# Block 4's gate and val by quarters as seven products in two shared PSUM banks, and sums of weights made from tiles already loaded

## Chip, cores and metric

One core of a Trainium2 chip. The metric is the time of one execution on the device in microseconds (us), the median of the runs shown. All data is fp32; a product of two fp32 matrices is made on TensorE from high and low parts (`float32r`): hi*hi + hi*lo + lo*hi, three matmuls.

## What is computed

Three stages over 3072 tokens of width 512 (batch 4, 8 heads, sequence 768, head size 64):

```python
# 1 retention, per head, gamma fixed by the head
state = gamma * state + outer(k[t], v[t]);  y[t] = scale * q[t] @ state
# 2 gated MLP, d_ff 1536
xn = x / sqrt(mean(x * x) + 1e-6) * rms_g
x2 = (silu(xn @ w_gate) * (xn @ w_val)) @ w_out
# 3 second MLP, d_ff 1024
h = x2 @ w_in;  solu = h * softmax(h)
out = layernorm(solu) * g_ln @ w_out2
```

## The kernel before

The tokens go in six blocks of 512 (`NB`), each through two stages on TensorE. The first stage makes gate, val and their output product over 12 pieces m of d_ff (`NM`), 128 wide; the second stage (`de_quarters` from block 2 on) is the second MLP, and ends with four output products (`e_mm`). While block n is in its first stage, the attention of block n + 1 runs between, in eight pieces (`att_pieces`: a score piece and an output piece for each of four chunks), in PSUM banks SB and YB. These pieces, the RMS norm of the next block, loads and other side work hang on numbered slots: `slot(n, s)` is called at slot 0 to 34 in the first stage (three to a piece m) and 35 to 57 in the second, and runs the functions that `extra` holds for it. Written order is not final: the planner of the framework orders each engine's instructions by its own times, within the ties that `issue_after` sets. Each engine, and SyncE's DMA queue, runs its instructions in that order.

In blocks 0 to 4 the first stage is `bc_block`: for each m, `gv` (L805) makes gate into bank GB and val into VB, each 4 k x 3 matmuls of 512 columns, `act_hl` (L814) multiplies silu(gate) by val and splits it, and `cmm` (L825) adds the output product of the piece before to the four banks X0 to X3, 12 matmuls. Weights are in DRAM as high and low part (`scr[m][part]`, 512 KB each; part 0 gate, 1 val, 2 output), written in block 0 and loaded again by `w_load` for each block: gate and val into four `w4` tiles, output weights into two `wo` tiles.

Block 5 (`SEVEN`) has another first stage, `seven_block` (L943). Two pieces m go together as a pair j, and each of gate and val is a 2 x 2 product of quarters (256 inputs or outputs by 256 tokens) by a Strassen-like scheme with seven products in place of eight. Each product is `seven_mm`, six matmuls of 256 columns (L913). Four products come in a first phase (`seven_1`) and three in a second (`seven_2`), into four quarters a, b | c, d: two halves of GB and two of VB for gate, SB and YB for val, since block 5 has no attention beside it. VectorE adds the quarters up between (L926 to L941, L973, L980). The products need sums of quarters of the weights and of the activations.

Sums of weights: for each j and part `sums_steps` (L586) loads two weight tiles, adds high and low part (L597), makes four sums on GpSimd (L605), splits them and stores them in DRAM (`sscr`), two loads and two stores of 512 KB. `SUMS_AT` puts these twelve jobs into block 2 (slots 17, 24), 3 and 4 (slots 1, 7, 13, 19, 25). `seven_load` and `seven_pump` fetch quarters and sums in tiles of a ring of ten and two.

Sums of activations: `x_sums` (L452) makes four differences in place in xT on GpSimd (L464), and their splits and those of three known quarters, in the slots 50 to 53 of block 4, that is beside its `e_mm`. The normalised activations live in xnh and xnl, where the second stage also keeps T weights that `t_load` brings. Low parts of these splits are made by GpSimd too (L101), high parts by ScalarE (L100).

Of the kernel before, what the change touches and what calls it, by code (L numbers as in the profile page):

```python
# [9 lines left out]
F32 = mybir.dt.float32  # L10
# [8 lines left out]
P = 128  # L19
# [16 lines left out]
SEVEN = (5,)  # L36
SUMS_AT = [(2, 17), (2, 24)] + [(n, 1 + 6 * i) for n in (3, 4) for i in range(5)]
# [5 lines left out]
def retention_moe_kernel(ctx: ExitStack, tc: tile.TileContext, qk0, q2, kt, kv, wpk, w2i, w2o,  # L43
# [395 lines left out]
    def rms_steps(bank, n):  # L439
        if n == 1:  # L440
            return [first(lambda: rms_1(bank)), first(lambda: rms_2(bank))] \
                + [first(lambda k=k: rms_mul(bank, k)) for k in range(NK)] \
                + [lambda k=k: xn_split(k) for k in range(NK)]
        norm = [rms_1t, lambda: rms_sum(bank), rms_2t] + [lambda k=k: rms_3t(k) for k in range(NK)]
        if n in SEVEN:
            return norm + x_sums()
        return norm + [lambda k=k: xn_split_t(k) for k in range(NK)]
# [4 lines left out]
    def x_sums():  # L452
# [10 lines left out]
        def sub(a, b, out):  # L463
            return lambda: nc.gpsimd.tensor_tensor(out=out, in0=a, in1=b, op=ALU.subtract)  # L464

        def summed(key, src, tag):
            def f():
                xs[key] = tuple(wt(tag, [P, 2, 256], F32R, 2) for _ in range(2))
                split(*xs[key], src, nc.gpsimd)
            return f  # L470

        k01, k23 = slice(0, 2), slice(2, 4)
        return [known("B11", k01, lo), known("B21", k23, lo), known("B22", k23, hi),
                sub(b12, b11, b11), sub(b22, b12, b12), sub(b22, b11, b22), sub(b21, b22, b21),
                summed("T2", b22, "rq"), summed("T3", b12, "rk"), summed("T1", b11, "kd"), summed("T4", b21, "qd")]
# [110 lines left out]
    def sums_steps(j, part):  # L586

        W, f, o = [], [], []

        def load():  # L590
            for m in (2 * j, 2 * j + 1):
                W.append(wt("x2", [P, 2, 512], F32, 4))
                nc.sync.dma_start(W[-1], scr[m][part])

        def whole():
            for w in W:
                nc.gpsimd.tensor_tensor(out=w[:, 0, :], in0=w[:, 0, :], in1=w[:, 1, :], op=ALU.add)  # L597

        def sums():
            a11, a12, a21, a22 = W[0][:, 0, lo], W[0][:, 0, hi], W[1][:, 0, lo], W[1][:, 0, hi]  # L600
            f.extend((st(), st()))
            s2, s3, s1, s4 = f[0][:, lo], f[0][:, hi], f[1][:, lo], f[1][:, hi]
            for out, a, b, op in ((s1, a21, a22, ALU.add), (s2, s1, a11, ALU.subtract),
                                  (s3, a11, a21, ALU.subtract), (s4, a12, s2, ALU.subtract)):
                nc.gpsimd.tensor_tensor(out=out, in0=a, in1=b, op=op)  # L605

        def parts():
            for t in f:
                o.append(wt("x2", [P, 2, 2, 256], F32R, 4))
                with tc.issue_after(recent["act"].ins), tc.issue_after(recent["dve"].ins):  # L610
                    split(o[-1][:, :, 0, :], o[-1][:, :, 1, :], t.rearrange("p (s x) -> p s x", s=2))

        def store():
            for i, t in enumerate(o):
                nc.sync.dma_start(sscr[j][part][:, 2 * i:2 * i + 2], t.bitcast(F32))

        def none():
            pass

        return [load, none, whole, sums, none, none, parts, none, store]  # L620
# [184 lines left out]
    def gv(g, part):  # L805
        w = wsp.pop((g, part))
        halves = [slice(0, 256), slice(256, 512)] if g == 0 else [slice(0, 512)]
# [17 lines left out]
    def cmm(g, m):  # L825
        w = wsp.pop((g, 2))
        ah, al = acts.pop(m)
        for d in range(NK):
            cs = slice(d * P, d * P + P)
            mm3(XB[d], w[:, 0, cs], w[:, 1, cs], ah, al, m == 0, m == NM - 1)  # L830
# [77 lines left out]
    def seven_mm(ps, w, key, start):  # L908
        h, l = xs[key]
        for k in range(2):  # L910
            cs = slice(k * P, k * P + P)
            for i, (x, y) in enumerate(((w[:, 0, cs], h), (w[:, 0, cs], l), (w[:, 1, cs], h))):
                nc.tensor.matmul(ps, lhsT=x, rhs=y[:, k, :], start=start and k + i == 0, stop=k == 1 and i == 2,  # L913
                                 skip_group_check=True)
# [28 lines left out]
    def seven_block(n):  # L943
        base = n * NM
        for j in range(NM // 2):
# [39 lines left out]
            if final:  # L985
                out(m - 1)
        t_load(0, n)
# [418 lines left out]
    for n in range(NB):  # L1406
        if n + 1 < NB:
# [4 lines left out]
            else:  # L1412
                begin, span, r = 0, 28, (30, 32, 33, 34, 34, 34, 34, 50, 50, 51, 51)
                extra.setdefault((n, 31), []).append(lambda n=n: t_load(0, n))
# [7 lines left out]
            if n + 1 in SEVEN:  # L1422
                r = (30, 32, 33, 34, 34, 34, 34, 50, 50, 50, 51, 51, 51, 51, 52, 52, 53, 53)
                first7 = [lambda: seven_load(n + 1)] \
                    + [lambda i=i: w_load((n + 1) * NM + i, 2) for i in range(2)] + [seven_pump]
                for s, f in zip((47, 48, 48, 51), first7):
# [7 lines left out]
            for i, (b, s) in enumerate(SUMS_AT):  # L1434
                if b == n:
                    for k, f in enumerate(sums_steps(i // 2, i % 2)):
                        extra.setdefault((n, s + k), []).append(f)
        (seven_block if n in SEVEN else bc_block)(n)
# [82 lines left out]
```

## Time and profile before

| | us |
|---|---|
| median of three runs | 981.66 |
| the runs | 974.83, 981.66, 981.83 |
| the profiled execution, whole | 975.58 |
| its span, first to last instruction | 973.5 |

The views name an instruction by engine and line: PE is TensorE's matmuls, PEld its weight loads, DVE VectorE, ACT ScalarE, POOL GpSimd, SPq SyncE's DMA queue. A matmul's own duration in a timeline includes its latency; what it costs in a stream is the distance between starts, which is also what the chain of waits gives. The granted clock of TensorE is 0.991 of full speed over the span.

### The profile page before, as it was taken

To read this page: it belongs to the slowest core of one execution; us is meant where nothing else is said; L and a number is where in the kernel's file an instruction comes from. 1 tells how busy PE (TensorE), PEld (TensorE's weight loads), DVE (VectorE), ACT (ScalarE), POOL (GpSimd) and SP (SyncE) were. 2 spreads that over 40 slices of the span, in tenths; PEclk is the share of its full clock that TensorE was granted. 3 is DMA by queue.
4 is the path that set the end of the run, shared out by engine and by line. 5 is a ranking of instruction groups with operands and counts; after the bars stand their busy time and mean duration, and the time that the engine had idled before them with its cause. 6 is when DMAs were issued, how large, how long until landed. Compare 5 with 4: busy or idle time off the path is not lost.

```text
span 973.5 us, 17543 instructions
## 1 busy us (share of the span) xinstructions
PE 957.4 (98%) x6636; PEld 797.4 (82%) x6636; DVE 522.9 (54%) x1036; ACT 407.8 (42%) x792; POOL 450.1 (46%) x490
## 2 busy tenths in 40 slices
PE   8899999999999999999999999999999999999998
PEld 7777887888887888888888888788888888999987
DVE  4787777563375653734473343475433366343473
ACT  3767655474244343322463222356222246321254
POOL 6886764683053484644535345627253336300022
PEclk8899999999999999999999999999999999999999
DMA  9699999896523305999823999932799953798501
GB/s 346 224 316 397 343 325 367 294 390 237 202 63 98 99 23 182 303 301 312 309 98 111 293 347 345 346 128 93 241 328 328 328 187 130 236 326 296 192 1 44
DMA packets 89044, 231.93 MB, mean 238 GB/s; under 512 B 11136, under 2 KB 28928, under 8 KB 87936
## 3 DMA queue, kind: packets, MB, share of 16 engines
q1 hardware_dynamic: 80176, 205.63, 63.1%
q10 hardware_dynamic: 8784, 25.17, 6.7%
q8 instruction: 53, 0.87, 0.4%
q14 instruction: 31, 0.25, 0.1%
HBM read 188.82 MB, written 41.94 MB: 237 GB/s over the span
## 4 chain that ended last, share of the span: by engine, by line
PE 82%; DMA 5%; POOL 5%; DVE 4%; ACT 3%; issue 1%; SPq 0%; ACTq 0%; POOLq 0%; DVEq 0%
PE X L801 9%; PE X L803 9%; PE X L802 9%; PE GB L801 6%; PE GB L803 6%; PE GB L802 6%; PE VB L801 5%; PE VB L802 5%; PE VB L803 5%; PE X L1184 3%; PE SB L121 3%; PE GB L1184 2%; PE VB L1184 2%; PE VB L913 2%; PE YB L913 2%; PE X L1043 1%
## 5 line engine op out<-in xcount | busy, mean ns | idle before, releaser
L802 PE MATMUL X<-r,wo 128*128 128x512 f32 x260 | 101.8, 392 | 0.0
L803 PE MATMUL X<-r,wo 128*128 128x512 f32 x260 | 101.2, 390 | 0.0
L820 DVE TENSOR_TENSOR f<-VB,f 128x512 f32<-128x512 f32 x60 | 41.3, 688 | 111.2 <-PE VB L803 96.0
L801 PE MATMUL X<-r,wo 128*128 128x512 f32 x260 | 99.1, 395 | 1.9 <-DMA wo<-scr 1.4
L100 ACT CAST r<-f 128x512 fp32r<-128x512 f32 x72 | 44.6, 620 | 130.5 <-DVE f L820 112.3
L702 POOL TENSOR_TENSOR st<-st,x 128x512 int32<-128x512 int32 x52 | 69.8, 1344 | 54.3 <-DVE st L701 19.3
L849 ACT ACTIVATE f<-GB 128x512 f32<-128x512 f32 x60 | 35.8, 596 | 129.7 <-PE GB L803 128.7
L801 PE MATMUL GB<-xnh,w 128*128 128x512 f32 (+1 forms) x220 | 86.9, 395 | 1.0 <-ACT xnh L403 1.0
L801 PE MATMUL VB<-xnh,w 128*128 128x512 f32 (+1 forms) x220 | 86.5, 393 | 0.0
L802 PE MATMUL GB<-xnl,w 128*128 128x512 f32 (+1 forms) x220 | 85.9, 391 | 0.3 <-DVE xnl L101 0.2
L803 PE MATMUL VB<-xnh,w 128*128 128x512 f32 (+1 forms) x220 | 85.5, 389 | 0.0
L802 PE MATMUL VB<-xnl,w 128*128 128x512 f32 (+1 forms) x220 | 85.5, 389 | 0.0
L803 PE MATMUL GB<-xnh,w 128*128 128x512 f32 (+1 forms) x220 | 85.4, 388 | 0.0
L101 DVE TENSOR_TENSOR r<-f,r 128x512 fp32r<-128x512 f32 x72 | 65.2, 907 | 31.3 <-ACT r L100 30.6
L281 POOL TENSOR_TENSOR U<-U,u 128x256 f32<-128x256 f32 x27 | 17.1, 631 | 100.3 <-PE YB L121 76.7
L101 POOL TENSOR_TENSOR r<-st,r 128x512 fp32r<-128x512 f32 x8 | 10.3, 1292 | 112.6 <-ACT r L100 112.6
L801 PEld LDWEIGHTS X<-r,wo 128*128 128x128 f32 x260 | 48.5, 188 | 12.8 <-issue 2.2
L801 PE MATMUL X<-w2oh,r 128*128 128x512 f32 (+1 forms) x144 | 56.7, 394 | 1.1 <-ACT f L1086 0.6
L802 PEld LDWEIGHTS X<-r,wo 128*128 128x128 f32 x260 | 48.8, 188 | 10.4 <-DVE r L101 0.4
L803 PEld LDWEIGHTS X<-r,wo 128*128 128x128 f32 x260 | 48.8, 188 | 10.2
L597 POOL TENSOR_TENSOR x<-x 128x512 f32<-128x512 f32 x24 | 31.0, 1296 | 54.3 <-DMA x<-scr 54.2
L803 PE MATMUL X<-w2oh,r 128*128 128x512 f32 (+1 forms) x144 | 55.8, 387 | 0.0
(456 smaller groups left out, 2538.7 us busy)
## 6 DMA issues: line engine op xcount, KB each, us to landing
w<-scr SPq DMA_DIRECT2D x96, 512.0 KB, 6.6
wo<-scr SPq DMA_DIRECT2D x59, 512.0 KB, 6.5
x<-in_wpk SPq DMA_DIRECT2D x36, 512.0 KB, 6.3
x<-scr SPq DMA_DIRECT2D x25, 512.0 KB, 7.5
sscr<-x SPq DMA_DIRECT2D x24, 512.0 KB, 8.6
rv<-in_kv SPq DMA_DIRECT2D x40, 256.0 KB, 6.3
scr<-CV ACTq DMA_DIRECT2D x18, 512.0 KB, 6.7
scr<-w ACTq DMA_DIRECT2D x12, 512.0 KB, 5.6
```

What stands on the lines that cost most here:

```text
L100: h = nc.scalar.copy(hi, src)
L101: (lo_eng or nc.vector).tensor_tensor(out=lo, in0=src, in1=hi.bitcast(F32), op=ALU.subtract)
L121: return lambda: nc.tensor.matmul(out, lhsT=lhsT, rhs=rhs, start=start, stop=stop)
L597: nc.gpsimd.tensor_tensor(out=w[:, 0, :], in0=w[:, 0, :], in1=w[:, 1, :], op=ALU.add)
L702: nc.gpsimd.tensor_tensor(out=ti, in0=ti, in1=lo, op=ALU.add)
L801: nc.tensor.matmul(ps, lhsT=lh, rhs=rh, start=start, stop=False)
L802: nc.tensor.matmul(ps, lhsT=lh, rhs=rl, start=False, stop=False)
L803: return nc.tensor.matmul(ps, lhsT=ll, rhs=rh, start=False, stop=stop)
L820: recent["dve"] = nc.vector.tensor_tensor(out=a, in0=GV[1], in1=silu[:, 0, :], op=ALU.mult)
L849: recent["act"] = nc.scalar.activation(s[:, 0, :], GV[0], AF.Silu)
L913: nc.tensor.matmul(ps, lhsT=x, rhs=y[:, k, :], start=start and k + i == 0, stop=k == 1 and i == 2, skip_group_check=True)
L1184: last["mm"] = nc.tensor.matmul(bank, lhsT=x[:, k, ts_], rhs=y[:, k, :], start=start and k + i == 0, stop=k == 1 and i == 2, skip_group_ch ...
```

## The change

Block 4 is put in `SEVEN`. `seven_block` stays for block 5; block 4 gets `shared_block`, in which gate and val take the four quarters of GB and VB in turn, with one output product between phase one and phase two from the second pair on. Its weights come by quarters through `fit`, a ring of six tiles (four `w4`, two `x2`), each of two products' weights, refilled by two DMAs of 256 KB as soon as its second product is issued. The last two output weights go to other tiles, and the T weights are loaded after the block.

Ten of the twelve sums of weights are made from the weight tiles that the block in progress has loaded for its own products (`kept`): (j 3 and 4) in block 2, (j 0 to 2) in block 3; j 5 still loads them, in block 3 at slots 17 and 23. None is left in block 4. They are made in place, and stored by four DMAs of 256 KB.

The differences of activations go to tiles of their own (`wo`) and are made at slot 35; their splits come at slots 39 to 42 for block 5, and at 51, 52, 52 and 55 for block 4. The output scaling of block 3's last `e_mm` is not put off to block 4's first slot any more.

```diff
-SEVEN = (5,)
-SUMS_AT = [(2, 17), (2, 24)] + [(n, 1 + 6 * i) for n in (3, 4) for i in range(5)]
+SEVEN = (4, 5)
+SUMS = {2: [(3, 0), (3, 1), (4, 0), (4, 1)], 3: [(0, 0), (0, 1), (1, 0), (1, 1), (2, 0), (2, 1)]}
+LATE_SUMS = {(3, 17): (5, 0), (3, 23): (5, 1)}
...
+        def subs():
+            for keys in (("T2", "T3"), ("T1", "T4")):
+                t = wt("wo", [P, 2, 2, 256], F32, 2)
+                raws.update((key, t[:, i]) for i, key in enumerate(keys))
+            for key, a, b in (("T1", b12, b11), ("T2", b22, raws["T1"]), ("T3", b22, b12), ("T4", b21, raws["T2"])):
+                nc.gpsimd.tensor_tensor(out=raws[key], in0=a, in1=b, op=ALU.subtract)
...
+        def whole(i):
+            w = kept.pop((2 * j + i, part))
+            if not X:
+                X.append(wt("x2", [P, 2, 512], F32, 4))
+            nc.gpsimd.tensor_tensor(out=X[0][:, i, :], in0=w[:, 0, :], in1=w[:, 1, :], op=ALU.add)
...
+        if resident:
+            at0, at1 = 6 * j + part, 6 * j + 3 + part
+            return {at0: [lambda: whole(0)], at1: [lambda: whole(1), sums], at1 + 2: [parts], at1 + 3: [store]}
+        return {0: [load], 2: [both, sums], 4: [parts], 5: [store]}
...
+        def mul(j, part, q, ps, key, start=False):
+            seven_mm(ps, stock.pop((j, part, q)), key, start)
+            at = 14 * j + 7 * part + q
+            if at % 2 and at // 2 + len(fit) < NT:
+                fit_load([at // 2 + len(fit)])
+
+        def phase1(j, part):
+            for q, ps, key in ((0, a, "B11"), (1, b, "T2"), (2, c, "T3"), (3, d, "T1")):
+                mul(j, part, q, ps, key, q in (0, 2))
+            y, t = f4(), st()
+            S.copy(t[:, hi], b)
+            V.tensor_tensor(out=t[:, lo], in0=a, in1=t[:, hi], op=ALU.add)
+            V.tensor_tensor(out=t[:, hi], in0=c, in1=t[:, lo], op=ALU.add)
+            V.tensor_tensor(out=y[:, 1, hi], in0=d, in1=t[:, hi], op=ALU.add)
+            return y, t
+
+        def phase2(j, part, y, t):
+            for q, ps, key in ((4, a, "B21"), (5, d, "B22"), (6, c, "T4")):
+                mul(j, part, q, ps, key)
+            V.tensor_tensor(out=y[:, 0, hi], in0=d, in1=t[:, lo], op=ALU.add)
+            V.tensor_tensor(out=y[:, 1, lo], in0=c, in1=t[:, lo], op=ALU.add)
...
+        for j in range(NM // 2):
...
+            g = phase1(j, 0)
+            slot(n, 6 * j)
+            if j:
+                out(m - 2, range(1) if final else range(NK))
+            slot(n, 6 * j + 1)
+            phase2(j, 0, *g)
...
+            silu = S.activation(gf[:, 256:], gf[:, 256:], AF.Silu)
+            slot(n, 6 * j + 2)
+            v = phase1(j, 1)
+            slot(n, 6 * j + 3)
...
+            elif j:
+                out(m - 1)
+            slot(n, 6 * j + 4)
+            phase2(j, 1, *v)
...
+            V.tensor_tensor(out=vf[:, lo], in0=a, in1=gf[:, lo], op=ALU.mult)
+            V.tensor_tensor(out=vf[:, hi], in0=vf[:, hi], in1=gf[:, hi], op=ALU.mult)
...
+            slot(n, 6 * j + 5)
...
+                r += (39, 40, 41, 42) if n + 1 == NB - 1 else (51, 52, 52, 55)
...
+        (seven_block if n == NB - 1 else shared_block if n in SEVEN else bc_block)(n)
```

## Rows read from the trace of the kernel before

**Rows 1.** The page, part 1: TensorE's busy time, share of the span, instructions.

```profile
PE 957.4 (98%) x6636; PEld 797.4 (82%) x6636; DVE 522.9 (54%) x1036; ACT 407.8 (42%) x792; POOL 450.1 (46%) x490
```

**Rows 2.** Waits of TensorE in blocks 3 to 5: us in total, times, longest.

```profile
PE X L801 <- DMA wo<-scr: 1.4, 1, 1.4
...
PE X L801 <- ACT f L1086: 0.6, 1, 0.6
...
PE GB L913 <- DVE st L926: 0.3, 1, 0.3
```

**Rows 3.** Windows: length, then busy time per engine, granted clock, DMA share, GB/s.

```profile
632.93:785.90 152.97, 152.97 (x1143) 125.54 (x1143) 73.60 (x155) 54.35 (x111) 66.54 (x78) 1.00 0.72 243
785.90:924.56 138.66, 137.72 (x861) 123.83 (x861) 69.66 (x167) 50.35 (x100) 26.95 (x36) 1.00 0.65 225
...
522.00:632.90 110.90, 109.50 (x897) 89.35 (x889) 43.01 (x81) 29.95 (x60) 50.07 (x54) 1.00 0.96 314
675.50:785.90 110.40, 110.40 (x942) 90.32 (x941) 43.76 (x81) 29.82 (x60) 46.17 (x52) 1.00 0.90 302
837.35:924.56 87.21, 87.21 (x601) 81.29 (x602) 39.12 (x91) 20.46 (x40) 0.00 (x0) 1.00 0.82 282
```

**Rows 4.** Timeline of TensorE, block 3: start, duration; twelve matmuls of 512 columns begin.

```profile
622.92 0.39 PE L801 MATMUL VB<-xnh,w 128*128 128x512 f32 x1
...
625.64 0.39 PE L801 MATMUL X<-r,wo 128*128 128x512 f32 x1
```

**Rows 5.** The chain of waits, block 5: start, length; 48 products' matmuls begin.

```profile
857.44 1.42 PE GB L913 x12
...
863.09 0.23 PE X L801
```

**Rows 6.** Timeline of TensorE, block 4: a score piece and an output piece.

```profile
675.79 0.27 PE L121 MATMUL SB<-rq,rk 64*64 64x64 f32 x1
...
676.65 0.66 PE L1043 MATMUL X<-ident,f 128*128 128x128 f32 x4
...
713.68 0.27 PE L121 MATMUL SB<-qd,U 64*64 64x64 f32 x1
...
715.01 0.50 PE L801 MATMUL VB<-xnh,w 128*128 128x512 f32 x1
```

**Rows 7.** Line 913's weight loads: duration in ns, min/median/max.

```profile
L913 PEld LDWEIGHTS VB<-qd,A x36: 187/188/192, 839.6 to 913.9; 128*128 128x128 f32 x36
```

**Rows 8.** Timeline of TensorE, block 5: a second phase's last product.

```profile
871.99 0.87 PE L913 MATMUL YB<-qd,A 128*128 128x256 f32 x6
872.70 0.28 PE L913 MATMUL GB<-xnh,x 128*128 128x256 f32 x1
```

**Rows 9.** Timeline of VectorE, the same stretch.

```profile
871.54 0.42 DVE L973 TENSOR_TENSOR f<-SB,f 128x256 f32<-128x256 f32 x1 [2.75 <-PE SB L913]
872.90 0.42 DVE L939 TENSOR_TENSOR f<-YB,st 128x256 f32<-128x256 f32 x1 [0.93 <-PE YB L913]
873.24 0.41 DVE L980 TENSOR_TENSOR f<-YB,st 128x256 f32<-128x256 f32 x1
...
874.67 0.69 DVE L101 TENSOR_TENSOR r<-f,r 128x512 fp32r<-128x512 f32 x1
```

**Rows 10.** Groups of VectorE in block 4 that are attention's.

```profile
L349 DVE TENSOR_REDUCE ssq<-sq 128x128 f32<-128x512 f32 x4 | 4.3, 1087 | 3.4 <-ACT sq L346 3.4
...
L278 DVE TENSOR_TENSOR U<-U,YB 64x128 f32<-64x128 f32 x14 | 4.0, 287 | 0.2
```

**Rows 11.** DMA issues in block 5: size, median us to landing.

```profile
w<-sscr SPq DMA_DIRECT2D x7, 256.0 KB, 5.2
```

**Rows 12.** The chain of waits, end of block 3.

```profile
620.13 9.66 DMA wo<-scr
```

**Rows 13.** Groups of GpSimd in block 3: the adds of a weight's parts.

```profile
L597 POOL TENSOR_TENSOR x<-x 128x512 f32<-128x512 f32 x8 | 10.3, 1289 | 23.1 <-DMA x<-scr 23.1
```

**Rows 14.** Timeline of GpSimd before block 5: the last split.

```profile
833.25 1.29 POOL L101 TENSOR_TENSOR qd<-xT,qd 128x512 fp32r<-128x512 f32 x1
```

More of the change, by code (lines that the diff above doesn't have):

```diff
@@ L584, in retention_moe_kernel @@
     recent = {}
-    def sums_steps(j, part):
-        W, f, o = [], [], []
-        def load():
[L591 to L597, printed above, removed]
-        def sums():
[L600 to L604, printed above, removed]
+    kept = {}
@@ new lines, in sums_steps, with both @@
+    def sums_steps(j, part, resident):
+        X, H = [], []
+        def whole(i):
[3 more added lines that the diff above has]
+            nc.gpsimd.tensor_tensor(out=X[0][:, i, :], in0=w[:, 0, :], in1=w[:, 1, :], op=ALU.add)
+        def load():
+            for t, m in ((X, 2 * j), (H, 2 * j + 1)):
+                t.append(wt("x2", [P, 2, 512], F32, 4))
+                nc.sync.dma_start(t[0], scr[m][part])
+        def both():
+            for i, w in ((0, X[0]), (1, H[0])):
+                nc.gpsimd.tensor_tensor(out=X[0][:, i, :], in0=w[:, 0, :], in1=w[:, 1, :], op=ALU.add)
+        def sums():
+            a11, a12, a21, a22 = (X[0][:, r, c] for r in range(2) for c in (lo, hi))
+            for out, a, b, op in ((a22, a21, a22, ALU.add), (a21, a11, a21, ALU.subtract),
+                                  (a11, a22, a11, ALU.subtract), (a12, a12, a11, ALU.subtract)):
@@ L617, in none @@
-        def none():
-            pass
-        return [load, none, whole, sums, none, none, parts, none, store]
+            if not H:
+                H.append(wt("x2", [P, 2, 512], F32, 4))
+            with tc.issue_after(recent["act"].ins), tc.issue_after(recent["dve"].ins):
+                for i in range(2):
+                    split(H[0][:, i, :].bitcast(F32R), X[0][:, i, :].bitcast(F32R), X[0][:, i, :])
+        def store():
+            for i, t in enumerate((H[0], X[0])):
+                for r, to in ((0, slice(0, 4, 3)), (1, slice(1, 3))):
+                    nc.sync.dma_start(sscr[j][part][:, to, i, :], t[:, r, :].rearrange("p (s x) -> p s x", s=2))
@@ L806, in gv @@
         w = wsp.pop((g, part))
+        if (g % NM // 2, part) in SUMS.get(g // NM, ()):
+            kept[g % NM, part] = w.bitcast(F32)
         halves = [slice(0, 256), slice(256, 512)] if g == 0 else [slice(0, 512)]
@@ L986, in seven_block, with fit_load, source @@
                 out(m - 1)
+        t_load(0, n)
+        with tc.issue_after(recent["wo"].ins):
+            t_load(1, n), t_load(2, n)
+        out(NM - 2)
+        out(NM - 1)
+    fit, stock = [], {}
+    def fit_load(tiles):
+        def source(j, part, q):
+            if q in (0, 4, 6):
+                return scr[2 * j + (q == 6)][part][:, :, lo if q == 0 else hi]
+            return sscr[j][part][:, (1, 2, 3, 5).index(q)]
+        for T in tiles:
+            t = fit[T % len(fit)]
+            for i in range(2):
+                key = ((2 * T + i) // 14, (2 * T + i) // 7 % 2, (2 * T + i) % 7)
+                nc.sync.dma_start(t.bitcast(F32)[:, i], source(*key))
+                stock[key] = t[:, i]
```

124 lines of the change are left out of this document (91 added, 33 removed).

## The prediction

> **What bounds the kernel now.** I read the page's first part, then who waits for whom on TensorE, then the windows by stage, then the chain of waits, whose pieces give the distance between starts in place of a matmul's whole latency. The page shows TensorE busy for 98% of the span [rows 1]. The waits say that this is work and not smeared idle time: over blocks 3 to 5 TensorE waited three times, 1.4, 0.6 and 0.3 us [rows 2]. The windows agree: in block 4 (675.5 to 785.9 us) and in block 5 (837.35 to 924.56) TensorE is busy for all of it at granted clock 1.00, while VectorE, ScalarE and GpSimd are each busy for less than half [rows 3]. So in block 4 the time is the number of matmuls times their pitch, and an edit of another engine or of a DMA is worth nothing until it makes TensorE wait. DMA is nearest to that: share 0.96 in block 3, 0.90 in block 4 [rows 3].
>
> **The products (the gain).** Block 4 now takes gate and val with 12 x 2 x 4 x 3 = 288 matmuls of 512 columns. Twelve of them start at 622.92 and the next instruction at 625.64: 2.72 / 12 = 0.2267 us each [rows 4], so 65.3 us. By sevens it is 6 pairs x 2 parts x 7 products x 6 = 504 matmuls of 256 columns. Block 5 already runs them: 48 in a row from 857.44 to 863.09, 5.65 / 48 = 0.1177 us [rows 5], so 59.3 us. The gain is 6.0 us. In columns it would be one eighth, 8.2 us; the short matmul gives some back, since 0.1177 is more than half of 0.2267. A check from whole stages: from the start of one second stage to the next it is 152.97 us with block 4 between and 138.66 with block 5 [rows 3], 14.31 apart. Block 4 has four chunks of attention more, each a score piece of 0.86 us and an output piece of 1.33 [rows 6], 8.76 in all, and block 5's stage holds 0.95 us of waits [rows 2]: 14.31 - 8.76 + 0.95 = 6.5. I take 6.0 and keep 6.5 as the other end.
>
> [...] Block 5's matmuls have a weight load each of 0.188 us [rows 7], those 48 together 9.0 us in a stretch of 5.65, so the loads lie beside the matmuls. [...] If loads stood in line, it would be 504 x (0.1177 + 0.188) = 154 us against 288 x (0.2267 + 0.188) = 119: 35 us lost. The trace disagrees; I keep 0.01 for it below.
>
> **The borders in shared banks (a new wait).** Block 5 has two sets of quarters (GB with VB, SB with YB). In block 4 SB and YB belong to block 5's attention, so gate and val use GB and VB in turn, and before each next group of products VectorE and ScalarE must have read the last one. The tightest place is from the last product of one part (into VB) to the first group of the next, where no output matmuls lie between: one border inside each of 6 pairs and one between pairs, 11. Block 5 shows the times. Its six products into the last quarter end where the next matmul starts, at 872.70 [rows 8], and the reads of that bank start at 872.90 and 873.24; the second ends at 873.65 [rows 9]. The products of the quarter that is read at 872.90 had all started before 871.99 [rows 8]: the read waited for the product beside it in the same bank. After a border two products go to GB first (12 x 0.1177 = 1.41 us, to 874.11 on this scale) before VB is written again: 0.4 us spare. GB is clear too, since its last quarter is read from 871.54, early [rows 9]. At the next step the parts for the output matmuls must be there: the low part's subtraction ends at 875.36 [rows 9], 2.66 after the border; block 4's output matmuls come four products later (2.82), and the low part is read first by the second of them, at 3.05. So without attention nothing waits, with 0.4 us to spare. Where no output matmuls cover the step from phase one to phase two (pair 0), an attention piece of 0.86 or 1.33 us lies there. What comes in front of these reads on VectorE is attention's work: 0.42 x 2 masks, 0.28 x 8 state adds and a 1.09 reduce a chunk, about 2.1 us a piece, eight pieces. If none lands before a border it costs 0; if each does, 8 x (2.1 - 0.4) = 13.8 us. The adds and the reduce are in [rows 10]; the masks have the shape of the quarters' adds in [rows 9]. I take 1.0, near the lower end, because VectorE is busy for 43.76 of 110.4 us [rows 3] and block 5, whose VectorE work is the same without attention, has no wait from 837.35 on.
>
> [...] By columns alone one quarter would be read before the last product ends, and 0.8 us would be spare at a border; by the bank it is 0.4: the trace shows the second.
>
> **The weights' quarters.** Each product pair takes a 512 KB tile from a ring of six, refilled by two 256 KB DMAs. From a tile's release to its next use ten products and at least one output pass: 10 x 0.706 + 12 x 0.2267 = 9.8 us (7.1 plus an attention piece in pair 0). Such a DMA lands in 5.2 us at the median in block 5 [rows 11]: some 4 us spare, less the time that SyncE takes to issue the two. Bytes: 36 refills and 12 output weights of 0.524 MB, 2.6 MB of attention, 3.1 of the second stage's T weights: 30.9 MB. Block 4 moved 302 GB/s x 110.4 = 33.3 MB [rows 3], with five pairs' sums that now leave it. So nothing waits: 0. The other end: at block 5's 282 GB/s [rows 3] 30.9 MB take 109.6 us where TensorE's share of that window would be 104.4: +5.2. A single row of a crowded queue speaks for it, 9.66 us to landing [rows 12].
>
> **The sums, blocks 2 and 3.** Ten of twelve are now made by GpSimd from the weight tiles that TensorE is using, and lose their 1 MB loads; two keep them. Block 3 held five sums of 4 x 0.524 MB, and holds six of half that and two whole: 10.5 MB both times, so its share of 0.96 stays. What moves is when: the last store leaves at slot 28, not 33, so the wait of 1.4 us at the block's end for output weights [rows 2, 12] may go. GpSimd gets three sums more, each two adds of 1.29 us [rows 13] and four of half width, between 2.6 and 7.7 us and about 5.2: 50.07 + 15.6 = 66 of 110.9 us, hidden, though a weight tile is held until its add is done. A weight load that is late for that costs about what the late one cost, 1.4 us; I take three such as the bad end. Value -0.7, ends -1.4 and +4.2.
>
> **The two seams.** For block 5 four subtractions and four splits leave the seam for the second stage before it, where GpSimd is idle for long. In the trace the last of these splits runs from 833.25 to 834.54 [rows 14], and TensorE's 0.95 us of waits [rows 2] stand behind that queue (the output scaling waits for GpSimd's small ops). I expect them gone. For block 4 four splits of 512 columns become seven: up to the same 0.95 comes in, I take 0.5. Net -0.45, ends -0.95 and +0.95. What is left (the T weights loaded after the block, its last two output weights in other tiles, the scaling for block 3 not put off) is covered by at least 8 us of output matmuls: 0.
>
> **The sum.** -6.0 + 1.0 + 0 - 0.7 - 0.45 = -6.15 us. The profiled execution took 975.58 us, its span of 973.5 and 2.1 around it: 969.4. The runs shown are 974.83, 981.66 and 981.83, so a run falls near 975 or near 982, and the profile is one of the first kind. I put the step on the middle of the profiled 975.58 and the median 981.66, 978.62: **972.5 us**.
>
> **The rivals.** (1) DMA becomes the bound in block 4: for it the share of 0.90 and the 9.66 us landing; against it block 5, which takes the same quarters at 0.82 without a wait, and fewer bytes than before. It gives back 5.2: 977.7. (2) VectorE's attention work stands before the borders, and the kernel gets slower: place, the 11 borders and the output matmuls behind them; price up to 13.8 in place of 1.0, so 972.5 + 12.8 = 985.3; it decides from (6.15 + 1.0) / 11 = 0.65 us a border. For it: spare time of 0.4 against a single reduce of 1.09. Against it: VectorE is idle for most of the block, and the planner may put these ops after the reads. (3) Block 3 gets crowded: +4.2 in place of -0.7, 977.4; for it DMA at 0.96. (4) Weight loads in line: +35 on the products, 1013; against it [rows 5, 7].
>
> **Chances.** Forecast 0.62 (its own range 967 to 976), (1) 0.16, (2) 0.13, (3) 0.08, (4) 0.01. The range: the best ends together, -6.5 - 1.4 - 0.95 = -8.85, from 975.58 give 966.7; above, rivals 1 and 3 on the upper of the two kinds of run, 981.66 - 1, and a part of rival 2: 967 to 983. One per cent, about what a measurement of this kernel can tell from no change, is 9.8 us, more than any case gains. It is passed only if the median of before stands on the upper kind and that of after on the lower, half of the forecast's 0.62: 0.30. Slower by over 1% needs rival 2 at its full price or rival 4: 0.06. Within 1%: 0.64.
>
> **What would show it.** Right: from the second stage of block 3 to that of block 4 it takes about 147 us where it was 152.97 [rows 3], 504 matmuls of line 913's kind in it at a pitch near 0.118, TensorE's waits in it under 2 us together, the block 3 and seam waits of rows 2 gone or smaller. Rival 1 shows as TensorE waiting for w or x tiles from scr and sscr; rival 2 as waits of the first VB product, or of output matmuls, for VectorE; rival 3 as waits for w in block 3. The forecast is wrong if block 4's stage shrinks by less than 3 us, or if its waits exceed 3.

## The result, and the profile after

The changed kernel takes 987.57 us (median of 14 runs, 980.21 to 992.36), the kernel before 978.26 beside it (14 runs): a ratio of 1.0094, 95% interval 1.007 to 1.0118. It is 0.9% slower, and outside the range of 967 to 983. The profiled execution after spans 985.8 us where that of before spans 973.5: 12.3 us apart where the medians are 9.3 apart, since the profiled execution of before is one of its shorter ones (975.58 us). The account below is of these two executions.

First the page of after, its part 1 and the DMA line of part 2 [rows 1]:

```profile
PE 959.8 (97%) x6852; PEld 805.7 (82%) x6852; DVE 562.9 (57%) x1102; ACT 413.1 (42%) x807; POOL 466.1 (47%) x497
...
DMA packets 109160, 230.92 MB, mean 234 GB/s; under 512 B 12176, under 2 KB 51472, under 8 KB 108048
```

TensorE has 216 matmuls more (504 short for 288 long), as intended, and is busy 2.4 us longer in a span 12.3 us longer. So something waits. The windows say where. A stage here runs from the first matmul of one second stage to that of the next; these are block 3's, 4's and 5's, then pieces of block 3's and one of the clock (columns as in [rows 3]). First the kernel before, for what [rows 3] does not hold:

```profile
478.32:632.76 154.44, 153.04 (x1127) 125.22 (x1126) 72.86 (x156) 54.53 (x111) 72.15 (x83) 1.00 0.77 256
478.00:522.00 44.00, 44.00 (x246) 36.26 (x248) 30.27 (x75) 24.97 (x51) 22.40 (x30) 1.00 0.29 111
522.00:560.00 38.00, 38.00 (x350) 31.07 (x345) 13.53 (x28) 10.50 (x21) 11.84 (x18) 1.00 0.84 253
560.00:600.00 40.00, 40.00 (x350) 32.61 (x340) 17.21 (x32) 10.31 (x23) 18.17 (x19) 1.00 1.04 341
```

and after:

```profile
477.99:639.91 161.92, 156.76 (x1128) 127.06 (x1126) 78.78 (x162) 57.83 (x117) 87.15 (x100) 0.98 0.75 242
639.91:797.67 157.76, 152.58 (x1360) 133.83 (x1358) 94.39 (x211) 55.59 (x118) 55.60 (x61) 0.99 0.75 235
797.67:936.57 138.90, 138.01 (x862) 123.31 (x860) 72.52 (x168) 49.04 (x99) 24.02 (x33) 1.00 0.66 221
478.00:522.00 44.00, 44.00 (x224) 36.24 (x226) 29.98 (x75) 24.00 (x50) 21.92 (x27) 1.00 0.20 78
522.00:560.00 38.00, 38.00 (x374) 30.84 (x370) 16.43 (x32) 13.46 (x26) 22.62 (x33) 1.00 0.79 239
560.00:600.00 40.00, 38.82 (x339) 31.28 (x330) 20.35 (x34) 11.35 (x24) 23.08 (x24) 1.00 1.04 345
607.30:613.00 5.70, 5.70 (x14) 4.46 (x15) 0.00 (x0) 0.14 (x1) 4.15 (x6) 0.50 1.06 359
```

Block 3's stage grew from 154.4 to 161.9 us, block 4's from 153.0 to 157.8 in place of shrinking by 6, block 5's by 0.2. The first 478 us take the same time in both (0.3 us apart). TensorE's waits in these three stages, after:

```profile
PE GB L824 <- DMA w<-scr: 4.9, 2, 3.7
PE X L1190 <- DVE r L1194: 2.5, 1, 2.5
PE X L825 <- DVE r L102: 1.2, 1, 1.2
PE GB L1331 <- POOL r L102: 0.7, 1, 0.7
PE YB L940 <- DMA w<-sscr: 0.7, 1, 0.7
PE VB L940 <- DVE f L1076: 0.3, 1, 0.3
PE X L824 <- ACT r L101: 0.3, 1, 0.3
PE GB L940 <- DVE f L1118: 0.2, 1, 0.2
```

Where [rows 2] had 2.3 us there are 10.8. The first line is block 3: TensorE waits for weights until 576.5 and until 607.3 us. The next three are the seam before block 4 (the end of block 3's second stage, where block 4's first products begin), block 4's end, and the start of the second stage before it. The fifth stands in the seam before block 5. The sixth and the last are borders of block 4's shared banks, the seventh is the end of block 3. And a wait can cost more than its length: behind that of 3.7 us, from 607.3 us on, the granted clock is 0.50 (the last window). Its 14 matmuls start within 5.7 us, and 13 distances of 0.2267 us [rows 4] would be 2.9.

The lengths of stages are steadier than whole times: but for e2 and e6, block 2's second stage starts between 473.5 and 481.9 us in the profiled executions, for reasons ahead of it. So the experiments are read by stages of the profiled execution, in us (start to start); beside them stands the median of all runs (for before, the medians beside the different runs; e6 has two runs, e8 three, e2 and e4 four, the others but e10 eight to fourteen):

```
                              block 3   block 4   block 5   median of runs
before                          154.4     153.0     138.7   977.0 to 979.0
after                           161.9     157.8     138.9   987.6
e1  sums only                   163.3     153.1     141.6   986.8
e2  sums not made               152.8     155.4     139.0   988.9
e4  wide stores                 162.4     156.5     138.6   989.4
e5  late splits                 164.3     154.9     138.9   986.3
e3  high parts elsewhere        158.3     157.8     138.9   986.1
e6  stores in place             153.3     155.7     139.0   991.4
e7  no late sums                154.4     156.6     139.3   981.0
e8  block 5 in shared banks     163.2     156.3     139.3   985.1
e10 late traffic alone          162.6     157.2     138.9   983.5 (one run)
e9a late sums early             154.3     156.4     138.7   978.0
e9b and subtractions pinned     153.5     153.8     138.8   973.4
e9c and norm pinned             153.9     152.3     139.0   973.9
e11 e9b with the old block 4    153.5     153.1     138.0   974.8
e9d e9b once more               153.4     153.3     138.2   974.3
```

### The profile page after: what moved, and what is told of

It is laid out like the page before. It is cut to its first block, busy times and chain, and to the rows that moved or that the text cites. A ratio compares the mean times of both kernels' runs of the same rounds, so it can differ in the third digit from the quotient of the medians.

```text
span 985.8 us, 18203 instructions
## 1 busy us (share of the span) xinstructions
PE 959.8 (97%) x6852; PEld 805.7 (82%) x6852; DVE 562.9 (57%) x1102; ACT 413.1 (42%) x807; POOL 466.1 (47%) x497
## 2 busy tenths in 40 slices
DMA packets 109160, 230.92 MB, mean 234 GB/s; under 512 B 12176, under 2 KB 51472, under 8 KB 108048
## 4 chain that ended last, share of the span: by engine, by line
PE 74%; DMA 10%; DVE 7%; POOL 4%; ACT 3%; issue 2%; SPq 0%; ACTq 0%; POOLq 0%; DVEq 0%
PE X L824 9%; PE X L825 9%; PE X L826 9%; PE VB L940 5%; PE GB L824 5%; PE GB L826 4%; PE GB L825 4%; PE VB L825 4%; PE VB L824 4%; PE VB L826 4%; PE GB L940 4%; PE SB L122 3%; DMA rv<-in_kv 3%; PE X L1331 2%; PE GB L1331 2%
## 5 line engine op out<-in xcount | busy, mean ns | idle before, releaser
L825 PE MATMUL X<-r,wo 128*128 128x512 f32 x252 | 99.8, 396 | 0.0
L826 PE MATMUL X<-r,wo 128*128 128x512 f32 x252 | 98.9, 393 | 0.0
L824 PE MATMUL X<-r,wo 128*128 128x512 f32 x252 | 95.5, 395 | 1.3 <-ACT r L101 1.3
L102 DVE TENSOR_TENSOR r<-f,r 128x512 fp32r<-128x512 f32 x72 | 69.8, 971 | 20.3 <-ACT r L101 19.4
L845 DVE TENSOR_TENSOR f<-VB,f 128x512 f32<-128x512 f32 x48 | 33.0, 688 | 80.3 <-PE VB L826 62.1
L824 PE MATMUL GB<-xnh,w 128*128 128x512 f32 (+1 forms) x172 | 68.7, 399 | 5.3 <-DMA w<-scr 4.9
L825 PE MATMUL GB<-xnl,w 128*128 128x512 f32 (+1 forms) x172 | 68.1, 396 | 0.5 <-DVE xnl L102 0.4
L826 PE MATMUL GB<-xnh,w 128*128 128x512 f32 (+1 forms) x172 | 67.7, 394 | 0.0
L824 PE MATMUL VB<-xnh,w 128*128 128x512 f32 (+1 forms) x172 | 67.4, 392 | 0.0
L825 PE MATMUL VB<-xnl,w 128*128 128x512 f32 (+1 forms) x172 | 66.8, 388 | 0.0
L826 PE MATMUL VB<-xnh,w 128*128 128x512 f32 (+1 forms) x172 | 66.5, 387 | 0.3 <-POOL w L102 0.3
L876 ACT ACTIVATE f<-GB 128x512 f32<-128x512 f32 x48 | 28.6, 596 | 90.1 <-PE GB L826 88.1
L824 PEld LDWEIGHTS X<-r,wo 128*128 128x128 f32 x252 | 47.0, 188 | 11.3 <-ACT r L101 1.8
L826 PEld LDWEIGHTS X<-r,wo 128*128 128x128 f32 x252 | 47.9, 190 | 10.0
L825 PEld LDWEIGHTS X<-r,wo 128*128 128x128 f32 x252 | 47.9, 190 | 10.0 <-DVE r L102 0.4
L825 PE MATMUL X<-w2ol,r 128*128 128x512 f32 (+1 forms) x144 | 55.8, 387 | 0.0
```

Of the source, the lines that this page charges most:

```text
L102: (lo_eng or nc.vector).tensor_tensor(out=lo, in0=src, in1=hi.bitcast(F32), op=ALU.subtract)
L824: nc.tensor.matmul(ps, lhsT=lh, rhs=rh, start=start, stop=False)
L825: nc.tensor.matmul(ps, lhsT=lh, rhs=rl, start=False, stop=False)
L826: return nc.tensor.matmul(ps, lhsT=ll, rhs=rh, start=False, stop=stop)
L845: recent["dve"] = nc.vector.tensor_tensor(out=a, in0=GV[1], in1=silu[:, 0, :], op=ALU.mult)
L876: recent["act"] = nc.scalar.activation(s[:, 0, :], GV[0], AF.Silu)
```

## Experiments on block 3

Line numbers are those of the changed kernel, a few lines further down in some runs. The diffs show the main lines, without casts. A sum of weights is resident when it is made from tiles that are loaded for the block's own products.

**e1, the sums alone.**

```diff
-SEVEN = (4, 5)
+SEVEN = (5,)
```

> Block 4 goes back to whole products in its own way; the sums from resident weights and block 5's part-splits put earlier stay. Theory H (block 3 is late because GpSimd's adds hold the weight tiles, and wait for buffers that are still being stored) and theory P (block 3 is late because the new stores leave in 1 KB pieces, 16 per partition and sum where there were 4 KB ones): block 3's stage, second stage to second stage, stays at 161 to 163 us against 154.4 before, block 4's goes back to 152.5 to 153.5, total 6 to 9 us over before. Theory B (what was lost lies in block 4 alone: its seam, its shared banks): block 3 at 154 to 155, total within 1.5 us of before.

Measured: 1.008 of before (1.0052 to 1.0108), block 3 at 163.3, block 4 at 153.1. The loss in block 3 belongs to the sums, not to block 4's form. Block 5's stage lost 3 us more, with waits of 1.1 and 0.7 us at the second stage's start, beside GpSimd's four subtractions, and of 1.4 for a tile of sums (after: 0.7).

**e2 and e6, stores without making.** A store takes its data from the second stage's weights:

```diff
-return {at0: [lambda: whole(0)], at1: [lambda: whole(1), sums], at1 + 2: [parts], at1 + 3: [store]}
+return {at1 + 3: [stored]}
```

> The change with the ten resident sums left out: no GpSimd add, no tile held, no split; the same stores (four DMAs of 256 KB in 1 KB pieces per sum, at the same slots) take their data from the second stage's weights, so blocks 4 and 5 multiply by wrong sums. The two loaded sums stay. Theory H: block 3's stage falls to 154 to 155.5, total 6.5 to 8 us under the changed kernel. Theory P: block 3 stays at 159 to 162, total at most 3 us under it. Block 4's stage is 157 to 158 by both.

> As the run without the making of the ten resident sums (their adds, splits and held tiles left out, blocks 4 and 5 multiply by wrong sums), with each store tied behind the gate and val matmuls of its slot, so that it leaves in block 2 or 3 where the changed kernel's store leaves, and not in block 1. Theory H: block 3's stage 152.5 to 155.5 us, no waits for weights over 1 us. Theory D: 158 to 162 us, since the bytes in block 3 are those of the changed kernel. Start of block 2's second stage back at 476 to 483 us by both.

Both missed their point. Having nothing to wait for, the planner sent the 40 stores out at 166 to 229 us, in block 1; the tie in e6 did not hold them back. There they delayed the weights so that TensorE was busy for 25.37 (e2) and 27.11 (e6) of the 35 us from 200 to 235 (before: 35.00), and the time is as bad as after's. What they do show: with neither adds nor stores of the ten sums in it, block 3 takes 152.8 and 153.3 us. They don't tell holding from traffic.

**e4, wide stores**, against the thought that the 1 KB pieces of the new stores are slow:

```diff
-for i in range(2): split(H[0][:, i, :], X[0][:, i, :], X[0][:, i, :])
+split(H[0][:, :, lo], H[0][:, :, hi], X[0][:, :, lo])
+split(X[0][:, :, lo], X[0][:, :, hi], X[0][:, :, hi])
...
+nc.sync.dma_start(S[:, 0:2], H[0])
+nc.sync.dma_start(S[:, 3], X[0][:, 0, :])
+nc.sync.dma_start(S[:, 2], X[0][:, 1, :])
```

> The change with the sums' parts laid side by side before they are stored, so that a sum leaves in one DMA of 4 KB pieces and two of 2 KB (384 packets) in place of four of 1 KB pieces (1024 packets); adds, holding and bytes as they are. Theory P: the moved rate at 590 to 603 us no longer falls to 210 to 260 GB/s, the two waits for weights in block 3 (1.3 and 3.8 us) go or shrink under 1 us in all, block 3's stage 155 to 157, total 5 to 7 us under the changed kernel. Theory H: block 3 within 1.5 us of 161.9, total within 2 us of the changed kernel.

Measured: 101288 DMA packets in place of 109160, block 3 at 162.4. The size of the pieces is not the cause.

**e3, high parts elsewhere.** The trace shows the holding that theory H is about. GpSimd in block 3, after; then the chain of waits there:

```profile
564.98 1.58 POOL L611 TENSOR_TENSOR x<-w 128x512 f32<-128x512 f32 x1 [6.89 <-DMA sscr<-x]
```

```profile
561.29 6.08 DMA sscr<-x
567.52 2.54 POOL x L611 x2
570.06 6.26 DMA w<-scr
576.45 0.47 PE GB L824
```

GpSimd stood idle for 6.89 us in front of an add that frees a weight tile (L611), until an earlier store landed and gave its x2 tile back. The chain shows the whole path: a store, two adds, a weight load that could leave only at 570.06, and TensorE, which waited for it until 576.45. The edit:

```diff
-H.append(wt("x2", [P, 2, 512], F32, 4))
+H[:] = wt("r2", [P, 512], F32, 8), wt("r2", [P, 512], F32, 8)
```

> The change with the high parts of a resident sum written to two half-size r2 tiles in place of an x2 tile, so that the two sums of one pair take two of the four x2 tiles and not all four, and the adds that read the weight tiles no longer wait for a store to land. Adds, bytes, stores and slots as they are. Theory H (the held weight tiles): GpSimd's waits for stores in front of its whole-width adds go, block 3's stage 154 to 156 us. Theory D (block 3 is bound by DMA in its second half: the sums from resident weights cannot start before their weights are there, so less is moved early, and the same bytes are pressed into less time): block 3's stage stays at 160 to 164 us.

Measured: 158.3, between the two. The wait that ended at 576.5 is gone, later ones stay. Its waits for weights in block 3:

```profile
PE GB L826 <- DMA w<-scr: 1.8, 1, 1.8
PE VB L826 <- DMA w<-scr: 0.9, 1, 0.9
```

**e7 and e10, the loaded pair.** e7 drops the two sums that are still loaded in block 3 (pair 5 then takes pair 4's), e10 drops only their adds and splits and moves the bytes as before:

```diff
# e7
-LATE_SUMS = {(3, 17): (5, 0), (3, 23): (5, 1)}
+LATE_SUMS = {}
# e10
-return {0: [load], 2: [both, sums], 4: [parts], 5: [store]}
+return {0: [load], 5: [store]}
```

> The change without its two loaded sums (pair 5): 4.2 of the 10.5 MB that the sums move in block 3 are gone; pair 5 reads pair 4's sums, so blocks 4 and 5 are wrong in that pair. The ten resident sums stay as they are. Theory D: 4.2 MB at 0.34 MB a us are 12 us of DMA time, the waits of block 3 go, its stage 153.5 to 156. Theory H: the wait near 575 us (1.3 to 1.9 us) stays, those after it may shrink: 156 to 160.

> The change with the making of pair 5's two loaded sums left out, but not their traffic: the 2.1 MB of weights are loaded at the same slots and stored as they came, so blocks 4 and 5 are wrong in that pair. Theory D (their 4.2 MB on the DMA queues delay the weights): block 3's stage stays at 159 to 164 us as in the changed kernel. Rival (their adds and splits on GpSimd, ScalarE and VectorE): 154 to 156.5 as in the run without these sums.

Measured: 154.4 without the traffic, 162.6 with the traffic and no work (e10 is one execution). Waits in block 3, first e7, then e10:

```profile
PE GB L824 <- DMA w<-scr: 0.8, 1, 0.8
```

```profile
PE GB L824 <- DMA w<-scr: 4.0, 2, 2.7
PE X L824 <- DMA wo<-scr: 1.8, 1, 1.8
...
```

So 4.2 MB of traffic in block 3's second half decide: theory D. The engines' work for these two sums costs nothing there that shows. Holding (H) is a part of the loss only while there is no room.

**e9a, both mended.** e3's tiles, and the loaded pair moved to the second stage of block 0, where DMA has room (share 0.13 from 345 to 370 us in the changed kernel):

```diff
-LATE_SUMS = {(3, 17): (5, 0), (3, 23): (5, 1)}
+LATE_SUMS = {(1, 62): (5, 0), (1, 63): (5, 1)}
```

> The change with two repairs of block 3's load: the high parts of resident sums in r2 tiles (as in the run before), and pair 5's two loaded sums made at slots 62 and 63 of block 1's list, in the second stage of block 0, where DMA is at 0.15 of its time, and not in block 3. All sums are made, nothing else moves. Theory D+H (late DMA bytes in block 3, and held tiles): block 3's stage 152.5 to 154.5 us where the changed kernel has 161.9, total 7 to 9 us under the changed kernel, which is level with before to 1 us under it. If block 3's loss had another cause, such as the number of stores from resident sums, its stage stays above 157.

Measured: block 3 at 154.3 without one wait for a weight, the total 0.9996 of before (0.9971 to 1.0022). All of block 3's loss is back.

## Experiments on block 4

**e5, late splits.** The seam before block 4, after: ScalarE and VectorE, each from its own timeline.

```profile
673.68 1.13 ACT L101 CAST x<-wo 128x512 fp32r<-128x512 f32 x2
...
674.71 0.58 ACT L1193 CAST r<-X 128x512 fp32r<-128x512 f32 x1
```

```profile
675.32 1.09 DVE L1176 TENSOR_TENSOR sm<-sm 128x1 f32<-128x1 f32 x1
...
677.82 1.27 DVE L1194 TENSOR_TENSOR r<-X,r 128x512 fp32r<-128x512 f32 x2
```

VectorE at the same place before, where the read (L1047) comes ahead of the row work (L1029):

```profile
666.23 0.67 DVE L1047 TENSOR_TENSOR r<-X,r 128x512 fp32r<-128x512 f32 x1
666.83 0.52 DVE L1029 TENSOR_TENSOR sm<-sm 128x1 f32<-128x1 f32 x1
```

Two casts of T2 and T3 (x<-wo) stand in front of the cast of the transposes' bank on ScalarE. VectorE's read of that bank (L1194) then comes behind the last chunk's row work instead of ahead of it, and TensorE's transposes into the bank wait for it: 2.5 us, with a granted clock of 0.50 from 678.5 to 681.6. The edit:

```diff
-r = (30, 32, 33, 34, 34, 34, 34, 35, 50, 50, 50)
-r += (39, 40, 41, 42) if n + 1 == NB - 1 else (51, 52, 52, 55)
+r = (30, 32, 33, 34, 34, 34, 34, 35 if n + 1 == NB - 1 else 47, 50, 50, 50)
+r += (39, 40, 41, 42) if n + 1 == NB - 1 else (54, 54, 56, 56)
```

> The change with GpSimd's four subtractions for block 4 moved from the start of block 3's second stage (slot 35) to slot 47, and the splits of the four sums of x from slots 51, 52, 52, 55 to 54, 54, 56, 56, behind the last chunk's row work. Theory S (the seam before block 4: ScalarE's casts and GpSimd's work for block 4's moving operands stand before the last chunk's transposes, TensorE idles 2.5 us and drops to half clock): the waits of 2.5 and 0.7 us go, block 4's stage from 157.8 to 152.5 to 154.5, total 3 to 5 us under the changed kernel. Theory R (the loss in block 4's stage lies in the block: shared banks and attention): stage at 156.5 or more, total within 1.5 us of the changed kernel. A new wait at block 4's first products for the late splits, up to 2 us, is possible with either.

Measured: the wait of 2.5 is 0.4, block 4's stage 154.9. The wait of 0.7 stayed: a later slot alone did not move the subtractions, which the planner still put from 644.6 to 650.6, ahead of the splits that the second stage needs.

**e8, shared banks without attention.** Block 5 by block 4's form, with its ring and its loads:

```diff
-(seven_block if n == NB - 1 else shared_block if n in SEVEN else bc_block)(n)
+(shared_block if n in SEVEN else bc_block)(n)
```

> The change with block 5 also in the shared-bank form: GB and VB in turn, the ring of quarters of block 4, though no attention runs in block 5 and its sums of x lie in whole tiles. Theory R1 (the borders of shared banks cost by themselves, some 24 places of 0.1 us or more): block 5's stage from 138.9 to 141 to 143 us. Theory R2 (they cost only where attention stands before the reads on VectorE): 138.5 to 139.5. Stages of blocks 3 and 4 as in the changed kernel, 161 to 164 and 157 to 158.5, by both.

Measured: 139.3, in the range of R2. Even so three border reads come late with no attention beside them: their distances lose 0.8 us, and the three right behind them 0.3. The stage grew by 0.4 alone, because the wait of 0.7 us for a tile of sums in the seam is gone. The pitch of the products away from breaks is 0.1182 us, as in block 5's own form.

**e9b, subtractions pinned.** The start of block 3's second stage, before: a VectorE operation, and the first low part that GpSimd makes for the second stage (S3).

```profile
637.09 0.69 DVE L1163 TENSOR_TENSOR r<-st,r 128x512 fp32r<-128x512 f32 x1
638.14 1.30 POOL L101 TENSOR_TENSOR r<-st,r 128x512 fp32r<-128x512 f32 x1 [5.40 <-ACT r L100]
```

After, with the last subtraction ahead of S3 and S4:

```profile
644.49 1.78 DVE L1310 TENSOR_TENSOR r<-st,r 128x512 fp32r<-128x512 f32 x1
645.69 1.74 POOL L471 TENSOR_TENSOR wo<-xT,wo 128x512 f32<-128x512 f32 x1
647.39 2.52 POOL L102 TENSOR_TENSOR r<-st,r 128x512 fp32r<-128x512 f32 x2
```

The edit ties the subtractions behind GpSimd's split of S4 (`recent["s4"]`), over e9a; they hang on slot 37, the splits on e5's slots:

```diff
-nc.gpsimd.tensor_tensor(out=raws[key], in0=a, in1=b, op=ALU.subtract)
+with tc.issue_after(recent["s4"].ins):
+    nc.gpsimd.tensor_tensor(out=raws[key], in0=a, in1=b, op=ALU.subtract)
```

> As that run, and GpSimd's four subtractions of x for blocks 4 and 5 tied behind its split of S4 in the second stage before, the splits for block 4 at slots 54, 54, 56, 56. Theory S (GpSimd's queue and the slowed VectorE at both ends of block 3's second stage): the waits near its start (0.9 us) and before its last transposes (2.65 us, and the half clock behind them) go; block 4's stage 153 to 154.5 where the changed kernel has 157.8; total 3 to 4.5 us under the run before, 3 to 5 under the kernel before the change. Theory R (shared banks): stage above 156.

Measured: both seam waits go (0.4 us is left of the larger; e5's splits go with it, so it is not the pin alone), block 4's stage at 153.8, the total 0.9942 of before (0.9913 to 0.997), the first version faster than the kernel before; once more as e9d, 0.9962 (0.9931 to 0.9992).

**e9c, the norm pinned**, over e9b. VectorE at block 4's end, after:

```profile
787.81 0.41 DVE L1076 TENSOR_TENSOR f<-VB,st 128x256 f32<-128x256 f32 x1
788.14 1.41 DVE L1119 TENSOR_TENSOR f<-f,f 128x256 f32<-128x256 f32 x1
789.48 1.78 DVE L1125 TENSOR_TENSOR f<-f,f 128x512 f32<-128x512 f32 x1
791.18 3.46 DVE L102 TENSOR_TENSOR r<-f,r 128x512 fp32r<-128x512 f32 x2
```

while GpSimd scales x by the norm:

```profile
786.73 5.66 POOL L428 TENSOR_TENSOR xT<-xT,ssq 128x512 f32<-128x512 f32 x4 [0.82 <-DVE ssq L425]
```

The edit, for block 5's norm (its scalings, subtractions and splits also move to slots 37 to 43):

```diff
+with tc.issue_after(recent["s4"].ins) if recent.get("pin") else nullcontext():
     nc.gpsimd.tensor_tensor(out=xT[:, k, :], in0=xT[:, k, :], in1=ssq, op=ALU.mult)
```

> As that run, and for block 5 the four scalings of x by the norm on GpSimd, which now run beside the last gate and val reads of block 4, tied behind the split of S4 in the second stage after it. Theory V (VectorE's operations with both operands in SBUF are slowed from 0.7 to 1.4 to 1.8 us while GpSimd computes): the wait of 1.2 to 1.4 us for the last r tiles of block 4 goes, VectorE's two last products take 0.4 and 0.7 us, block 4's stage falls by 1 to 2 us; up to 2 us of it may come back in the second stage before block 5, where GpSimd then has 5.6 us more. Rival: the slow operations are slow by their operands, and stay at 1.4 to 1.8 us.

Measured, the last three of these lines with GpSimd idle:

```profile
778.06 0.42 DVE L1123 TENSOR_TENSOR f<-f,f 128x256 f32<-128x256 f32 x1
778.39 0.68 DVE L1129 TENSOR_TENSOR f<-f,f 128x512 f32<-128x512 f32 x1
779.17 1.35 DVE L102 TENSOR_TENSOR r<-f,r 128x512 fp32r<-128x512 f32 x2
```

Theory V holds: the same shapes take 0.42 for 1.41, 0.68 for 1.78, 1.35 for 3.46 us. The wait of 1.2 at block 4's end is gone and the stage is 152.3, 1.5 under e9b's. The stages around are 0.6 longer, and the total, 0.9946 (0.991 to 0.9982), is not told apart from e9b's. GpSimd's scaling beside them is four operations of 1.4 us, and not all that VectorE does there is slower: 0.42 us of work on two inputs in SBUF took 1.41, while the read of PSUM ahead of it (L1076, VB) kept its 0.41. Why the one engine slows the other no run shows.

In e9b and e9c TensorE also waits in the middle of block 4 for a tile of sums, 1.1 and 1.2 us. In e9b's waits and its chain:

```profile
PE VB L943 <- DMA x<-sscr: 1.1, 1, 1.1
721.44 7.50 DMA x<-sscr
```

The tile lands 7.5 us after its issue, where 5.2 was the median [rows 11]. (For e9c the profile names a VectorE operation on the other bank. In e9d that operation comes behind the same product, so the product does not wait for it.)

**e11, the old block 4 in the mended kernel** (`SEVEN = (5,)` over e9b).

> The repaired kernel (sums, pinned subtractions) with block 4 back in its old form, whole products of 512 columns. Theory N (block 4's new form is worth nothing even when its side costs are mended: 6.0 us of products against some 3 us at its borders, 0.9 of a longer pitch and 1.4 at its end): block 4's stage 152.5 to 153.5, block 3's 153 to 154.5, total within 2 us of the repaired kernel, and so under the kernel before as well, by the sums and the seams alone. Theory G (the new form does give time): total 3 us or more over the repaired kernel, level with before.

> The repaired kernel once more (sums as from the run with early late sums, subtractions pinned), beside its twin with the old block 4 on the same chip: total 973 to 975, 0.99 to 0.997 of before; block 4's stage 153.5 to 154.5, block 3's 153 to 154.5.

Measured side by side: 974.81 us (0.998 of before, 0.9957 to 1.0003) with the old block 4, 974.27 with the new, 12 runs each, not told apart; block 4's stage 153.1 and 153.3. Block 4's windows, old form, then new form:

```profile
630.88:783.97 153.09, 153.09 (x1143) 125.61 (x1142) 66.00 (x146) 49.32 (x101) 38.80 (x48) 1.00 0.56 178
```

```profile
634.47:787.77 153.30, 150.57 (x1359) 132.85 (x1358) 92.20 (x212) 54.80 (x116) 48.30 (x55) 1.00 0.79 244
```

Theory N: with block 3's load and the seam mended, the new form is worth nothing that shows. (The wait at block 4's end, 1.3 us, is still in e9d; e9c is without it and has 152.3 us for block 4's stage, but no shorter total than e9b.) The work is 6 us less, but VectorE is busy for 92 us where it was 66, and TensorE waits for 2.7 us and takes longer between its products. The old form waits for nothing.

## Why the prediction was wrong, step by step

To price the steps I take each distance between starts over 0.1177 us (256 columns) and 0.2267 (512) in block 4's stage as lost. The rest of that stage is small matmuls, of attention and transposes, some 11.2 us in both. Before, 153.0 is 149.9 of work and 3.0 lost; after, 157.8 is 144.0 and 13.8: 10.8 more.

- **Products, -6.0: right but for the pitch.** The numbers of matmuls are those of the sum. Away from all breaks block 4's products come every 0.1196 us and not every 0.1177, which gives 0.9 back. Loads in line, rival 4's 35 us, no run shows: block 4's matmuls keep this pitch with a load of 0.19 us each. Block 5's own mean was 0.1183 before, so the 48 of [rows 5] were a good stretch; why block 4's is longer still was not tried, and by e8 (0.1182) it is not the shared banks alone.
- **Borders, +1.0: mis-sized, 2.1.** Beside the pitch the products' distances lose 3.2 us. 1.1 are three late reads (waits of 0.3, 0.2 and under 0.1 us). 2.1 are 23 distances of 0.16 to 0.23 us. Eleven of these lead into a piece of attention or out of one, and the old form loses as much there: 0.09 us before each of the eight pieces and 0.11 behind, 1.5 us in either kernel. Three come right behind the late reads, nine stand in the seam and in the last pair: with the late reads 2.1 us are new. A change of bank costs nothing by itself, as the step held: 25 of 29 changes from one product to the next in the other bank take 0.119 or 0.120 us. Rival 2's mechanism is there. VectorE, after, ahead of the border reads that TensorE waited for until 705.07 and 738.81:

```profile
703.27 1.08 DVE L350 TENSOR_REDUCE ssq<-sq 128x128 f32<-128x512 f32 x1 [0.56 <-ACT sq L347]
...
704.59 0.42 DVE L1076 TENSOR_TENSOR f<-VB,st 128x256 f32<-128x256 f32 x1
...
736.33 0.42 DVE L300 TENSOR_TENSOR A<-SB,mtab_t 128x256 f32<-128x256 f32 x1 [2.74 <-PE SB L122]
...
737.12 0.59 DVE L279 TENSOR_TENSOR U<-U,YB 64x128 f32<-64x128 f32 x2
737.72 0.58 DVE L279 TENSOR_TENSOR U<-U,SB 64x128 f32<-64x128 f32 x2
738.34 0.42 DVE L1118 TENSOR_TENSOR f<-GB,f 128x256 f32<-128x256 f32 x1
```

  A reduce of 1.08 us stands in front of one, masks and state adds of 2 us in front of the other, just as rival 2 put it. But it happens at three borders, and costs 0.2 to 0.5 us each; its price of 13.8 was far off (8 x (2.1 - 0.4) is 13.6). That its total of 985.3 lies near the 987.6 is luck.
- **The weights' quarters, 0: right.** After has no wait in block 4 for them. Rival 1's mechanism shows at one place in later runs, 0.4 to 1.2 us (e5, e9b, e9c, e9d).
- **The sums, -0.7: the step that failed most, +7.5.** "10.5 MB both times, so its share of 0.96 stays. What moves is when" took the moving for a gain at the block's end. But a loaded sum can be fetched any time ahead, one from a resident weight not before that weight. So DMA moves 78 GB/s where it moved 111 from 478 to 522 us, and 239 for 253 to 560: 44 x 33 + 38 x 14 = 1984 KB less, which has to follow where the share is above 1.0 in both kernels. At 0.345 MB a us that is 5.7 us, an estimate near the 7.5. e10 and e7 show that without the loaded pair's traffic the loss is gone, and that its work plays no part; e3 shows the held tiles to be a part of it. That these 2 MB are what tipped it was not tried by itself. Rival 3 named this mechanism, and capped it at 4.2 by counting a late load as 1.4 us: neither the queue behind it nor the clock of 0.50 was in that price.
- **The seams, -0.45: wrong sign.** The start and the end of block 3's second stage lost 1.7 and 4.5 us, where before lost 0.0 and 0.4: +5.8. The step counted GpSimd's splits; it missed their casts on ScalarE, in front of the transposes' cast (e5), and the subtractions at slot 35, whose work the planner drew ahead of S3 and S4 and beside which VectorE is slower (1.78 us for 0.69, e9b). Block 5's waits of 0.95 went, but its seam has a new one of 0.7 us for a tile of sums.
- **Not in the sum: block 4's end, +1.5.** The old form's last product reads PSUM, and took 0.69 us beside GpSimd's scaling; the new one's two read SBUF twice, and took 1.41 and 1.78 beside it, 0.42 and 0.68 without it (e9c). The prediction has no term for it; the block 5 that it went by has no GpSimd work beside it [rows 3]. e9c takes it back.

Pitch, borders, seam and end are 0.9 + 2.1 + 5.8 + 1.5 = 10.3 of the 10.8; the rest is in small pieces. Together by stages: 7.5 + 4.8 + 0.2 = 12.5 us, -0.3 ahead of them: the 12.3 between the spans.

"The forecast is wrong if block 4's stage shrinks by less than 3 us, or if its waits exceed 3" was the right test: it grew by 4.8, with about 5 of waits.

## What to carry to other kernels

Equal bytes are not an equal load: ask from when on each transfer may start, and whether the windows before are the idle ones. Block 3's mean share of DMA was 0.77 before, but 1.04 from 560 to 600 us, and with some 2 MB more left for that half (the estimate above) its stage took 7.5 us more. Work handed to an idle engine is not free if a step on another engine stands ahead of it (the high parts' casts, a wait of 2.5 us) or if a third is slower beside it (VectorE's 0.42 us that took 1.41 beside GpSimd). When TensorE is busy for 98%, a cut in its matmuls pays only while every other engine's deadline keeps its slack: here 6.0 us less work bought as much in waits and longer distances.

## What was unexpected of the hardware

- After TensorE's wait of 3.7 us the granted clock was 0.50 for the next 5.7 us (2.7 us lost). In blocks 3 to 5 of all runs shown, the mean over the next 5 us was 0.50 after two waits of 3.7 us, 0.66 to 0.69 after eleven of sixteen waits of 2.1 to 2.7 us and 1.00 after the other five, and 1.00 after six of 1.6 to 1.8. The same wait of 2.5 us in the seam before block 4 was followed by such a lower clock (after: 0.68) in six runs and not in e2, e6 and e8.
- VectorE's two-input operations on SBUF took 2.6 to 3.4 times as long beside GpSimd's (0.42 to 1.41, 0.68 to 1.78 us, e9c).
- On both sides of a piece of attention the distance between TensorE's starts was longer with nothing to wait for, 0.09 us before and 0.11 behind, after matmuls of 512 and of 256 columns alike.
- 1 KB or 2 to 4 KB pieces of a store made no difference that shows to its stage (e4: 162.4 us, after: 161.9).
